# Eight PSUM banks shared out anew and a hand-written order re-timed in an attention-plus-FFN kernel

## The chip, the cores and the metric

The kernel runs on one core of a Trainium2 chip. The metric is the device time of one launch in microseconds (us), the median of the runs. Names of engines are those of the profile: PE is the matrix engine, PEld its weight load, DVE, ACT and POOL the vector, scalar and GpSimd engines, SP the queue that issues most of the DMAs here. L12 is line 12 of the kernel before, unless the text says that a line is of the changed one.

## The reference

Eight batches of eight heads, 1024 positions and head dimension 64 go through an attention with projected keys and values, and its output, as 8192 tokens of 512, through a feed-forward layer:

```
k_proj = np.einsum('ks,bhsd->bhkd', E, k)          # E, F: 64 x 1024
v_proj = np.einsum('ks,bhsd->bhkd', F, v)
attn   = softmax(q @ k_proj^T / sqrt(64))          # over the 64 projected keys
x      = (attn @ v_proj) as 8192 x 512
h      = x @ w_in                                  # 512 x 2048
g      = h * sigmoid(1.702 * h)
out    = g @ w_out                                 # 2048 x 512
```

## The kernel before, in words

The tokens are worked off in 16 blocks of 512 (two to a batch). For each block PE does FFN1, 16 tiles of 4 matmuls (`ffn1`, L412, matmul L418), each tile evacuated by ACT with the gelu (L420) into `gT`, and then FFN2. Block 0's FFN2 is plain (`ffn2`, L422). From block 1 on, FFN2 is done with seven products of half matrices in place of eight (`ffn2_parts`, L467, matmul L485): sums of halves of `w_out` are made once on DVE (`w_sums`, L446, tiles `tw`) and sums of halves of `gT` once a block on DVE (`g_sums`, L457, tiles `sg`). The seven products are 14 parts of 8 matmuls each, numbered 0 to 13 here. They accumulate in three banks of PSUM, `g0`, `g1`, `g2`: products 1 and 2 in `g0`, 6, 7 and 4 in `g1`, 5 and 3 in `g2`. Partial sums are taken out of a bank in the middle: after product 7 (part 9) DVE adds `g1` to a saved sum into the output tile (L528), and product 4, which comes next, goes on adding in the same bank, so that its first matmul must wait for that read.

The attention of later blocks is woven into this work: `scores` (matmul L266, exp on ACT L285), `sums` (the softmax denominators, matmul L304, copied to `den` by DVE L307), `gather` and `spread` (the denominators go through DRAM to be re-laid: den to `rc` L315, reciprocal L323, `rc` to `rdr` L325, `rdr` to `rbc` in two DMAs L328, all issued by SP), `values` (matmul at L266's helper, multiplied by `rbc` on DVE L350 into `xT`). For blocks 1 and 2 another form is used: `tok` (L390, reciprocal L395, multiply L397) and `x_tr` (transposes L405, copy L406). A batch's projection is `proj` (L177), its copies `kv_out` (L225 to L226: `k_b`, then a transposing DMA into `kt`), and `q_dma` (L256) transposes q by DMA. `load` issues a batch's k, v and q loads on POOL's queue; each of these tensors has one buffer, freed by the batch before.

PSUM has eight banks. `ps_f` has five buffers for all of FFN1, scores, sums, values, tok, x_tr and proj; `ps_g` has the three named banks. `f_tile` takes a `ps_f` buffer; until FFN2 of block 1 (the `opening`), `x_any` instead takes `g0`, `g1`, `g2` in turn for attention work.

Nothing is scheduled by a tool: the order is written by hand. `at(j, slot, f)` puts step f of the attention behind FFN1 tile `slot` of block j, or for slots from `O` (16) on, behind a part of FFN2 that the table `SLOT` (L637) names. Every engine and queue works through its instructions in this order; a step waits where its tile or buffer is not free.

## Time and profile before

| | us |
|---|---|
| median of 16 runs | 506.34 |
| lowest of the runs | 504.25 |
| the profiled execution's own time | 504.25 |
| its span, first to last instruction | 502.5 |
| PE busy | 484.2 |
| ACT busy | 275.5 |
| DVE busy | 202.6 |
| POOL busy | 81.0 |

The profiled execution is 2.1 us below the median, and 1.75 us of its time lie outside its span. A matmul's row in the timeline shows a start and a length; the lengths overlap, since matmuls are pipelined, so the distance between the starts of two rows tells more than the gap that is shown between them.

### The profile page before, as it was taken

How to read it: one execution, taken by the hardware profiler on the slowest of the kernel's cores; microseconds unless marked ns; L12 is line 12 of the kernel's file. 1: busy time of each engine (PE TensorE's matmuls, PEld its weight loads, DVE VectorE, ACT ScalarE, POOL GpSimd, SP SyncE). 2: the span in 40 equal slices, each digit the busy share in tenths (PEclk: the TensorE clock that was granted, in tenths of full speed). 3: DMA queues.
4: the chain of work that ended last, by engine and by line, in shares of the span. 5: the costliest groups of instructions: out<-in, count | busy, mean ns of one | idle time of the engine just before them, and what ended most of it. 6: DMA issues, size and time to landing. Idle time of an engine off the chain costs nothing.

```text
span 502.5 us, 8738 instructions
## 1 busy us (share of the span) xinstructions
PE 484.2 (96%) x3707; PEld 298.1 (59%) x3707; DVE 202.6 (40%) x434; ACT 275.5 (55%) x444; POOL 81.0 (16%) x100
## 2 busy tenths in 40 slices
PE   8999989997999999999999999999999999999996
PEld 4644447565475665747566574757557475756665
DVE  4413875334243444424243532433453242334241
ACT  1664364663656646575565646566465647554351
POOL 7562060320600330005100060000000000000000
PEclk9999999999999999999999999999999999999999
DMA  9999999999998999189982899447230505032202
GB/s 167 200 190 208 210 153 176 199 225 133 191 201 203 158 121 254 27 190 127 200 165 87 168 97 235 97 146 109 93 85 3 168 1 165 8 119 52 85 0 85
DMA packets 131548, 69.09 MB, mean 137 GB/s; under 512 B 98229, under 2 KB 122805, under 8 KB 129589
## 3 DMA queue, kind: packets, MB, share of 16 engines
q0 software_dynamic: 86496, 29.37, 53.7%
q1 hardware_dynamic: 44932, 38.90, 31.2%
q8 instruction: 29, 0.48, 0.4%
q10 hardware_dynamic: 80, 0.26, 0.3%
q14 instruction: 11, 0.08, 0.0%
HBM read 72.88 MB, written 16.99 MB: 179 GB/s over the span
## 4 chain that ended last, share of the span: by engine, by line
PE 83%; DMA 7%; DVE 5%; ACT 2%; issue 1%; POOL 1%; SPq 0%; DVEq 0%; POOLq 0%
PE f_ps L418 39%; PE g_ps L485 35%; PE f_ps L266 2%; PE f_ps L430 2%; DMA rbc<-rdr 2%; PE f_ps L177 2%; ACT expT L285 2%; DMA q_even<-in_q_dram 2%; DMA kt<-k_b 2%; DMA rdr<-rc 1%; DVE x_sb L397 1%; PE f_ps L304 1%; DVE o_sb L453 0%; DVE tw L454 0%; POOL k_sb L57 0%
## 5 line engine op out<-in xcount | busy, mean ns | idle before, releaser
L418 PE MATMUL f_ps<-xT,w_in_sb 128*128 128x512 bf16 (+1 forms) x1032 | 224.4, 377 | 0.0
L420 ACT ACTIVATE gT<-f_ps 128x512 bf16<-128x512 f32 (+1 forms) x258 | 153.2, 594 | 79.1 <-PE f_ps L418 78.9
L418 PEld LDWEIGHTS <-w_in_sb 128*128 128x128 bf16 x1032 | 100.7, 98 | 116.7 <-issue 0.8
L485 PEld LDWEIGHTS <-sg 128*128 128x128 bf16 x960 | 92.7, 98 | 16.2 <-DVE sg L465 5.2
L485 PE MATMUL g_ps<-tw,sg 128*128 128x256 bf16 x720 | 83.8, 273 | 0.0
L485 PEld LDWEIGHTS <-gT 128*128 128x128 bf16 x720 | 69.3, 98 | 17.3 <-issue 6.3
L462 DVE TENSOR_TENSOR sg<-gT 128x1024 bf16<-128x1024 bf16 (+2 forms) x45 | 23.0, 512 | 119.5 <-ACT gT L420 119.5
L69 POOL DMA_DIRECT2D q_sb<-in_q_dram x48 | 42.0, 906 | 167.2 <-DMA qT<-q_sb 141.7
L485 PE MATMUL g_ps<-w_out_sb,gT 128*128 128x256 bf16 x480 | 57.6, 273 | 0.0
L285 ACT ACTIVATE expT<-f_ps 128x512 bf16<-128x512 f32 (+1 forms) x60 | 31.6, 583 | 24.0 <-PE f_ps L266 23.8
L350 DVE TENSOR_TENSOR xT<-f_ps,rbc 128x512 bf16<-128x512 f32 x52 | 33.4, 684 | 26.9 <-DMA rbc<-rdr 19.6
L528 DVE TENSOR_TENSOR o_sb<-g_ps,u_sb 128x512 f32<-128x512 f32 x15 | 10.4, 691 | 64.1 <-PE g_ps L485 42.6
L533 ACT COPY o_sb<-g_ps 128x512 f32<-128x512 f32 x15 | 8.8, 585 | 41.2 <-PE g_ps L485 41.2
L485 PE MATMUL g_ps<-tw,gT 128*128 128x256 bf16 x240 | 28.8, 273 | 1.6 <-DVE o_sb L528 1.6
L485 PE MATMUL g_ps<-w_out_sb,sg 128*128 128x256 bf16 x240 | 28.6, 273 | 0.0
L507 ACT COPY u_sb<-g_ps 128x512 f32<-128x512 f32 x30 | 17.7, 589 | 14.4 <-ACT u_sb L507 8.1
L463 DVE TENSOR_TENSOR sg<-sg,gT 128x1024 bf16<-128x1024 bf16 (+2 forms) x45 | 23.1, 514 | 1.6
L538 DVE TENSOR_TENSOR o_sb<-g_ps,u_sb 128x512 f32<-128x512 f32 x15 | 10.4, 692 | 32.9 <-PE g_ps L485 32.9
L464 DVE TENSOR_TENSOR sg<-gT 128x1024 bf16<-128x1024 bf16 (+2 forms) x45 | 22.8, 506 | 0.0
L465 DVE TENSOR_TENSOR sg<-gT,sg 128x1024 bf16<-128x1024 bf16 (+2 forms) x45 | 22.8, 506 | 0.0
L289 ACT ACT_TABLE_LOAD x15 | 19.2, 1283 | 0.3
L499 ACT COPY g_ps<-g_ps 128x512 f32<-128x512 f32 x15 | 8.6, 570 | 18.6 <-PE g_ps L485 17.1
(103 smaller groups left out, 294.0 us busy)
## 6 DMA issues: line engine op xcount, KB each, us to landing
out_dram<-o_sb SPq DMA_DIRECT2D x15, 1024.0 KB, 4.1
rbc<-rdr SPq DMA_DIRECT2D x26, 512.0 KB, 7.3
k_sb<-in_k_dram POOLq DMA_DIRECT2D x7, 1024.0 KB, 13.1
v_sb<-in_v_dram POOLq DMA_DIRECT2D x7, 1024.0 KB, 18.1
q_sb<-in_q_dram POOLq DMA_DIRECT2D x48, 128.0 KB, 5.7
w_in_sb<-in_moe_w_in_dram POOLq DMA_DIRECT2D x8, 256.0 KB, 11.1
w_out_sb<-in_moe_w_out_dram POOLq DMA_DIRECT2D x4, 512.0 KB, 11.5
q_even<-in_q_dram POOLq DMA_DIRECT2D x12, 128.0 KB, 13.3
```

What stands on the lines that cost most here:

```text
L69: nc.gpsimd.dma_start(out=qt[b][:, j], in_=qv[:, j])
L285: nc.scalar.activation(expT[h][:, 2 * u + i, ts], s_ps[i], AF.Exp, scale=scale)
L289: nc.scalar.preload_act_table(AF.Gelu_apprx_sigmoid)
L350: nc.vector.tensor_tensor(x_of(h)[:, 2 * u + i, :], n_ps[i], rbc[h][:, 2 * u + i, :], op=ALU.mult)
L418: nc.tensor.matmul(h_ps, w_in_sb[:, kc, fc * P:(fc + 1) * P], xT[j][:, kc, ts], start=(kc == 0), stop=(kc == KC - 1))
L420: nc.scalar.activation(gts[j][:, fc, ts], h_ps, AF.Gelu_apprx_sigmoid)
L462: tt(t[0], g[:, lo, THI], g[:, hi, THI], op=ALU.add)
L463: tt(t[1], t[0], g[:, lo, TLO], op=ALU.subtract)
L464: tt(t[2], g[:, lo, TLO], g[:, lo, THI], op=ALU.subtract)
L465: tt(t[3], g[:, hi, TLO], t[1], op=ALU.subtract)
L485: nc.tensor.matmul(gb[bank[i]][:, tc_], a[:, k, tc_ * P:(tc_ + 1) * P], w[:, k], start=(first and tc_ == 0 and k == 0), stop=(final and k ...
L507: nc.scalar.copy(u[n], gb[n])
```

## The change

It shares out the banks anew. `ps_f` has four buffers in place of five, and there is a fourth named bank `g3`. In the opening `x_any` turns through four named banks in place of three. After the opening every fifth `f_tile` is `g3`, so that five banks still go round. The second of the two tiles of `sums` is now always `g0`.

It moves steps. The six DVE instructions of `w_sums`, all at block 1's tile 0 before, go one to block 0's piece 10, three to its last piece, two to block 1's tile 6. Block 2's `tok` and its `x_tr`, woven into block 1's FFN2, have two parts of FFN2 between them in place of one; batch 2's `q_dma` goes from part 7 of that FFN2 to part 6; `sums(3)` and `gather(3)` go from block 2's tile 3 to block 1's part 11, `spread(3)` from tile 6 to tile 0 and from SP's queue to POOL's; the loads of batch 3 go behind it. Batch 2's projection goes from tile 3 to tile 1 of block 2, batch 3's from block 2's FFN2 to block 3's tile 3, and its `q_dma` to block 3's tile 2. The slots from `O` on now count parts directly; `O + 1`, `O + 6`, `O + 9` and `O + 11` are the parts where `O`, `O + 3`, `O + 6` and `O + 7` were, so that most steps stay where they stood.

It changes the last block. Product 7 comes before the second half of product 2. Products 5 and 3 go, by halves of the tokens, into two `f_tile`s, and the last sum and its output are two pieces of 128 tokens.

The core of the diff:

```diff
-    ps_f = ctx.enter_context(tc.tile_pool(name="ps_f", bufs=5, space=PSUM))
+    ps_f = ctx.enter_context(tc.tile_pool(name="ps_f", bufs=4, space=PSUM))
...
+    opening, f_next, g_next = [True], [0], [0]
+
     def f_tile(shape, dt=F32):
+        if not opening[0]:
+            f_next[0] += 1
+            if f_next[0] % 5 == 0:
+                return ps_g.tile(shape, dt, name="g3_ps")
         return ps_f.tile(shape, dt, name="f_ps")
...
-        return ps_g.tile(shape, dt, name=f"g{g_next[0] % 3}_ps")
+        return ps_g.tile(shape, dt, name=f"g{g_next[0] % 4}_ps")
...
-            d_ps = [x_any([P, TB]) for _ in range(2)]
+            d_ps = [x_any([P, TB]), ps_g.tile([P, TB], F32, name="g0_ps")]
...
-    def spread(h):
+    def spread(h, q=nc.sync):
...
-            nc.sync.dma_start(out=rdr.rearrange("p e (r n) -> (p e r) n", n=n), in_=rc)
+            q.dma_start(out=rdr.rearrange("p e (r n) -> (p e r) n", n=n), in_=rc)
...
-                nc.sync.dma_start(out=rbc[h][r], in_=rdr[None, :, e, :].to_broadcast([D, HP, TB]))
+                q.dma_start(out=rbc[h][r], in_=rdr[None, :, e, :].to_broadcast([D, HP, TB]))
...
+        def p3l(tc_):
+            def go():
+                for k in range(FH):
+                    nc.tensor.matmul(gl[tc_][:, :MH], sg[:, 3, k, tc_ * P:(tc_ + 1) * P], b22[:, k],
+                                     start=False, stop=(k == FH - 1), skip_group_check=True)
+                nc.vector.tensor_tensor(o[:, tc_, MH:], gl[tc_][:, :MH], u[1][:, tc_], op=ALU.add)
+                put(slice(tc_, tc_ + 1), slice(MH, DM))
+            return go
...
+        if last:
+            return [p1a, p1b, p5l(0), p5l(1), h(6, 0), p6b, h(2, 0), h(7, 0), p7b, p2b, h(4, 0), p4b, p3l(0), p3l(1)]
...
-    at(1, 0, w_sums)
+    for i, f in enumerate(w_sums()):
+        at(*((0, Q + 10), (0, Q + 13), (0, Q + 13), (0, Q + 13), (1, 6), (1, 6))[i], f)
...
-    at(2, 3, sums(3), gather(3), proj(2), kv_out(2, nc.scalar.copy))
-    at(2, 6, spread(3))
...
+    at(1, O + 11, sums(3), gather(3))
+    at(1, O + 6, q_dma(2))
+    at(2, 0, spread(3, nc.gpsimd), lambda: load(3))
+    at(2, 1, proj(2), kv_out(2, nc.scalar.copy))
...
+    at(3, 2, q_dma(3))
+    at(3, 3, proj(3), kv_out(3))
...
-    SLOT = {1: 0, 3: 1, 5: 2, 6: 3, 7: 4, 8: 5, 9: 6, 11: 7}
```

**PE, behind part 9 of block 3's FFN2**, stands here with the buffers' numbers (weight loads and repeats left out); `f_ps` is a `ps_f` buffer, `g0_ps` and `g3_ps` are named banks. Before:

```order
L485 MATMUL g1_ps_1735<-tw_202,sg_203 128x256
L266 MATMUL f_ps_1834<-qT_1393,kt1_130 32x512
L266 MATMUL f_ps_1835<-qT_1393,kt1_130 32x512
L266 MATMUL f_ps_1846<-expT_1395,vq0_131 32x512
L266 MATMUL f_ps_1847<-expT_1395,vq0_131 32x512
L304 MATMUL f_ps_1858<-expT_1516,ones_137 32x512
L304 MATMUL f_ps_1859<-expT_1516,ones_137 32x512
L485 MATMUL g1_ps_1735<-tw_202,gT_1602 128x256
```

And in the changed kernel:

```order
L493 MATMUL g1_ps_1735<-tw_202,sg_203 128x256
L270 MATMUL g3_ps_1834<-qT_1603,kt1_130 32x512
L270 MATMUL f_ps_1835<-qT_1603,kt1_130 32x512
L270 MATMUL f_ps_1846<-expT_1393,vq0_131 32x512
L270 MATMUL f_ps_1847<-expT_1393,vq0_131 32x512
L308 MATMUL f_ps_1858<-expT_1514,ones_137 32x512
L308 MATMUL g0_ps_1859<-expT_1514,ones_137 32x512
L493 MATMUL g1_ps_1735<-tw_202,gT_1578 128x256
```

The order is the same. Before, six tiles went through five banks, so the sixth took the bank of the first, which ACT must have read; now the sixth is in `g0`.

**SP's queue, from block 1's FFN2 to block 3.** `qT`, `kt` are the transposing DMAs, `rc`, `rdr`, `rbc` the denominators' way, `out_dram` a block's output. Before:

```order
L256 DMA_TRANSPOSE qT<-q_even 128x32x128
L542 DMA out_dram<-o_sb 128x2048
L315 DMA rc<-den 128x1x32
L226 DMA_TRANSPOSE kt_129<-k_b 128x4x64
L325 DMA rdr<-rc 128x32
L328 DMA rbc<-rdr 64x4x512 x2
L256 DMA_TRANSPOSE qT<-q_sb 128x32x128
L315 DMA rc<-den 128x1x32
L226 DMA_TRANSPOSE kt_130<-k_b 128x4x64
L542 DMA out_dram<-o_sb 128x2048
```

And in the changed kernel:

```order
L260 DMA_TRANSPOSE qT<-q_even 128x32x128
L319 DMA rc<-den 128x1x32
L547 DMA out_dram<-o_sb 128x2048
L230 DMA_TRANSPOSE kt_129<-k_b 128x4x64
L319 DMA rc<-den 128x1x32
L547 DMA out_dram<-o_sb 128x2048
L329 DMA rdr<-rc 128x32
L332 DMA rbc<-rdr 64x4x512 x2
L260 DMA_TRANSPOSE qT<-q_sb 128x32x128
L230 DMA_TRANSPOSE kt_130<-k_b 128x4x64
```

Block 3's denominators (the first `rc`) are gathered ahead of block 1's output, and their `rdr` and `rbc` have left this queue. Batch 3's q transpose and `kt_130` now stand behind the next block's `rdr` and `rbc`.

**DVE, from the end of block 0 to batch 1's key copy.** `tw` and `o_sb` are the tiles of `w_sums`, `k_b` the copy of the projected keys. Before:

```order
L406 COPY xT<-g_ps 128x256 x2
L450 TENSOR_TENSOR tw<-w_out_sb 128x2048
L451 TENSOR_TENSOR tw<-w_out_sb 128x2048
L452 TENSOR_TENSOR o_sb<-w_out_sb 128x2048
L453 TENSOR_TENSOR o_sb<-o_sb,w_out_sb 128x2048
L454 TENSOR_TENSOR tw<-w_out_sb,o_sb 128x2048
L455 CAST tw<-o_sb 128x2048
L225 CAST k_b<-f_ps 64x512
```

And in the changed kernel, from the first of these sums on:

```order
L459 TENSOR_TENSOR tw<-w_out_sb 128x2048
L410 COPY xT<-g_ps 128x256 x2
L399 RECIPROCAL rd<-g_ps 128x4
L401 TENSOR_TENSOR x_sb<-g_ps,rd 128x256
...
L410 COPY xT<-g_ps 128x256 x2
L459 TENSOR_TENSOR o_sb<-w_out_sb 128x2048
L459 TENSOR_TENSOR tw<-w_out_sb 128x2048
L459 TENSOR_TENSOR o_sb<-o_sb,w_out_sb 128x2048
L229 CAST k_b<-f_ps 64x512
```

One sum stands ahead of the last two token copies of block 1, three behind them, and two (not shown) behind `k_b`.

## The prediction

> **What bounds the kernel now.** The page comes first, then PE's waits.

> ```profile
> PE 484.2 (96%) x3707; PEld 298.1 (59%) x3707; DVE 202.6 (40%) x434; ACT 275.5 (55%) x444; POOL 81.0 (16%) x100
> ```

> ```profile
> PE f_ps L304 <- ACT expT L285: 2.8, 10, 0.3
> ...
> PE f_ps L405 <- DVE x_sb L397: 1.0, 4, 0.3
> PE g_ps L266 <- ACT expT L285: 0.8, 2, 0.5
> PE g_ps L390 <- DVE xT L406: 0.5, 3, 0.2
> ```

> PE is the bound, and the change keeps its matmuls. So it can gain only what PE loses between them, and the second view names places: total, times, longest. These figures are too small: a matmul's row is drawn to its modelled end, and part of a wait lies under it. I therefore work from distances between starts, with 0.217 us for a matmul of 512 columns (the L418 group under rival 3: 224.4 us for 1032) and half of that for 256, so 0.87 for an FFN1 tile and for a part of FFN2.

> **The change part by part.** *Sums in `g0`, blocks 3 to 12.* PE behind part 9 of block 3 and of block 13 (which has no scores left to do), then of block 4, where a projection follows; start, length, what, count, idle before:

> ```profile
> 149.03 0.41 PE L266 MATMUL f_ps<-qT,kt 64*32 64x512 bf16 x8
> ...
> 150.12 0.41 PE L304 MATMUL f_ps<-expT,ones 64*32 64x512 bf16 x7 [0.28 <-ACT expT L285]
> 150.46 1.92 PE L485 MATMUL g_ps<-tw,gT 128*128 128x256 bf16 x16
> ...
> 439.43 0.41 PE L266 MATMUL f_ps<-expT,vq 64*32 64x512 bf16 x8
> ...
> 440.35 0.82 PE L485 MATMUL g_ps<-tw,gT 128*128 128x256 bf16 x6 [0.30 <-DVE o_sb L528]
> ```

> ```profile
> 178.37 0.41 PE L304 MATMUL f_ps<-expT,ones 64*32 64x512 bf16 x7 [0.28 <-ACT expT L285]
> 178.85 0.38 PE L177 MATMUL f_ps<-k_sb,eft 128*64 128x512 bf16 x1
> ```

> In block 3 the fill takes 150.46 - 149.03 = 1.43 us, because the sixth tile takes the bank of the first score tile and waits for its exp. With that tile in `g0`, whose last reader (the copy of product 2) is two parts back, the wait goes. What is late next is DVE's read of `g1`: block 13 has no exp wait, and product 4 still comes 440.35 - 439.43 = 0.92 us behind part 9. So a fill costs 0.92 and gains 0.51. There are ten such waits, 2.8 us in all, in blocks 3 to 12. In the four with a projection (4, 6, 8, 10) the projection is the sixth tile of the five banks and waits for the first exp, no longer the second: 178.85 less the start that the first exp allows, about 178.25 (where the row at 178.37 stands, whose wait that exp ends), gains 0.6. Sum: 6 x 0.51 + 4 x 0.6 = **5.5** (4.5 if the projections gain half of it; 6.1 if all ten gain 0.6).

> *Opening.* The two score waits on a named bank (0.8 us, 2) and the three of `tok` (0.5, 3) go with a fourth bank. The row behind one of them, and the sum that now stands ahead of two copies in DVE's queue:

> ```profile
> 39.84 0.40 PE L266 MATMUL g_ps<-qT,kt 64*32 64x512 bf16 x4 [0.48 <-ACT expT L285]
> ```

> ```profile
> 53.79 1.22 DVE L450 TENSOR_TENSOR tw<-w_out_sb 128x2048 bf16<-128x2048 bf16 x1
> ...
> 64.33 0.67 DVE L225 CAST k_b<-f_ps 64x512 bf16<-64x512 f32 x1
> ```

> I add 0.15 to each shown wait for what lies under the rows: 1.3 + 5 x 0.15 = 2.05. Against it, DVE reaches the last tokens' multiplies later; two pieces of FFN2 lie between, so of 1.22 us I let 0.4 show (bounds 0 and 1.22). Four `ps_f` banks in the opening cost nothing: a gelu takes less time than a tile's matmuls (rival 3). **1.65** (0.8 to 2.3).

> *The wait for batch 1's keys.* PE, and SP's queue:

> ```profile
> 71.00 1.91 PE L485 MATMUL g_ps<-w_out_sb,gT 128*128 128x256 bf16 x16
> 74.29 0.62 PE L266 MATMUL f_ps<-qT,kt 64*32 64x512 bf16 x16 [1.38 <-DMA kt<-k_b]
> ...
> 89.84 3.62 PE L418 MATMUL f_ps<-xT,w_in_sb 128*128 128x512 bf16 x16
> ...
> 112.81 0.40 PE L266 MATMUL f_ps<-qT,kt 64*32 64x512 bf16 x4
> 116.16 0.40 PE L266 MATMUL f_ps<-qT,kt 64*32 64x512 bf16 x4 [2.95 <-DVE xT L350]
> 116.75 0.41 PE L266 MATMUL f_ps<-expT,vq 64*32 64x512 bf16 x8 [0.20 <-DVE xT L350]
> ...
> 125.73 13.98 PE L418 MATMUL f_ps<-xT,w_in_sb 128*128 128x512 bf16 x64
> ```

> ```profile
> 57.67 5.26 SPq L256 DMA_TRANSPOSE qT<-q_sb  x1
> 65.02 1.84 SPq L226 DMA_TRANSPOSE kt<-k_b  x1
> ...
> 84.30 7.43 SPq L256 DMA_TRANSPOSE qT<-q_even  x1
> ...
> 95.18 0.70 SPq L315 DMA_DIRECT2D rc<-den  x1
> ...
> 104.03 1.32 SPq L328 DMA_DIRECT2D rbc<-rdr  x2
> ```

> `k_b` (64.33) stood behind all six sums; now it comes at once. But SP is busy with q's transpose until 57.67 + 5.26 = 62.93, so `kt` can go out at most 2.1 us sooner, while PE arrives 1.65 sooner. With the same time in flight the wait shrinks by 0.45. **0.5** (0 to 1.5, the whole wait, 74.29 - 71.00 - 16 x 0.109).

> *Block 2's tokens.* Each of the four visits in block 1's FFN2 waits for DVE:

> ```profile
> 82.91 0.28 PE L405 MATMUL f_ps<-ident,x_sb 128*128 128x128 bf16 x2
> 83.45 0.28 PE L405 MATMUL f_ps<-ident,x_sb 128*128 128x128 bf16 x2 [0.26 <-DVE x_sb L397]
> ```

> The second pair starts 0.54 behind the first and needs some 0.11, so 0.4 is lost, four times: 1.6. With two parts between, the multiplies are done. But behind part 9 the new order puts two transposes, a `tok` and all of `scores(3)` in a row on five banks, behind L528 in DVE's queue; I take 0.3 off. **1.3** (0.6 to 1.7).

> *Block 3's values.* The rows at 112.81, 116.16 and 116.75 show block 2's PE waiting for a bank that the `values` multiply holds until `rbc` lands: four of these matmuls take 0.11, so 116.16 - 112.92 and 116.75 - 116.27 less 0.1, together **3.6**. The sums now come two parts ahead of block 2 and not four tiles into it: 6 x 0.87 = 5.2 us sooner against PE's work. But SP transposes batch 2's q first, from 84.30 (when that q has landed) for 7.43 us, so `rc` cannot go before 91.7 less the 1 us by which I take that q to land sooner: 90.7 against 95.18, 4.5 sooner, while PE is 3.45 sooner (the three parts above). That alone leaves 2.5 of the wait. But from `rc` to `rbc` it took 104.03 - 95.18 = 8.9 while batch 3's loads ran; they now stand behind, and I estimate 6. So the wait goes, and three small ones come: product 4's DVE wait in block 2, whose fill loses its projection (0.37, by block 13's rows); the projection of batch 2 at tile 1 meeting its v load; DVE's copies behind the reciprocal. For v, its issue and its time to landing:

> ```profile
> 76.80 0.87 POOL L57 DMA_DIRECT2D v_sb<-in_v_dram  x1 [1.27 <-PE g_ps L485]
> ...
> 95.94 0.88 POOL L57 DMA_DIRECT2D k_sb<-in_k_dram  x1 [18.27 <-PE f_ps L177]
> ```

> ```profile
> v_sb<-in_v_dram POOLq DMA_DIRECT2D x1, 1024.0 KB, 11.9
> ```

> It landed at 88.7; PE now arrives at 89.84 - 3.45 + 2 x 0.87 = 88.1, with the load itself some 1 us sooner. I take 0.3 for it, 0.3 for the copies, 0.4 for batch 3's projection (rival 2). 3.6 - 1.4 = **2.2** (0 to 3.6).

> [...]

> ```profile
> L69 POOL DMA_DIRECT2D q_even<-in_q_dram x12: 873/890/1513, 19.8 to 74.6; - x12
> ```

> One issue took 1513 ns against a median of 890. [...]

> *Last block.* PE waits for L528 between products 7 and 4, and the last sum spans 512 columns:

> ```profile
> 494.89 1.91 PE L485 MATMUL g_ps<-tw,gT 128*128 128x256 bf16 x16 [0.84 <-DVE o_sb L528]
> ...
> 498.58 0.69 DVE L538 TENSOR_TENSOR o_sb<-g_ps,u_sb 128x512 f32<-128x512 f32 x1 [3.75 <-PE g_ps L485]
> ```

> ```profile
> out_dram<-o_sb SPq DMA_DIRECT2D x15, 1024.0 KB, 4.1
> ...
> out_dram<-o_sb SPq DMA_DIRECT2D x4, 256.0 KB, 2.3
> ```

> Product 2's second half, 8 matmuls, now covers DVE's 0.69: 0.84 gained. The last sum halves, 0.35. The last transfer halves from 256 KB; on a line through the two sizes shown that is worth 1.8 x 128 / 768 = 0.3 (bounds 0 and 1.15). **1.5** (0.8 to 2.3).

> **Sum.** 5.5 + 1.65 + 0.5 + 1.3 + 2.2 + 1.5 = 12.65. The profiled execution took 504.25 us (span 502.5): 491.6. It lies 2.1 below the median of 506.34; the same gain there gives **493.7**.

> **Rivals.** *1. The loads keep the clock.* The gains before block 3 are worth something only if the DMAs come earlier too. Batch 2's q and v follow `proj(1)`, but they also share the engines with everything else; if they land at the same time as before, the gains up to block 2's start (3.45) are lost again at its projection and its `rc`, and what stays is 5.5 + 1.5 + some 1.3 of block 2: 8.3, **498**. For it: `kt` and v both show PE within 1 us of a landing. Against: v's issue hangs on PE's `proj(1)` through POOL's order.

> *2. Batch 3 is late.* POOL now issues batch 3's loads behind `rbc(3)`, 3 to 6 us later than at 95.94, and its projection is needed at block 3's tile 3:

> ```profile
> v_sb<-in_v_dram POOLq DMA_DIRECT2D x1, 1024.0 KB, 17.3
> ```

> From about 98 to 102, plus 17.3, plus up to 3.5 for `rbc`'s own megabyte ahead of it, v lands at 115 to 123; PE is there at about 121.3 (block 3 began at 125.73; less 3.45, the 2.6 that block 2 saves by then and the projection's 16 x 0.109, plus four tiles). Then come q's transpose and `kt(3)`, behind `rdr(4)` and `rbc(4)` on SP, and `scores(6, 0)` wants them some 25 us into block 3. Price 3 to 5 us: **498**. [...]

> *3. Slower.* With four banks in the opening FFN1 could wait for ACT in blocks 0 and 1. A tile's matmuls take 4 x 0.217 = 0.87 us and a gelu 0.59:

> ```profile
> L418 PE MATMUL f_ps<-xT,w_in_sb 128*128 128x512 bf16 (+1 forms) x1032 | 224.4, 377 | 0.0
> L420 ACT ACTIVATE gT<-f_ps 128x512 bf16<-128x512 f32 (+1 forms) x258 | 153.2, 594 | 79.1 <-PE f_ps L418 78.9
> ```

> To eat 12.65 us, each of 34 tiles would have to lose 0.37, that is, a bank's round trip would have to exceed 4 x 0.87 = 3.5 us. At 0.8 a tile 34 x 0.8 = 27 less 12.65 makes **521**. The rows give a round trip near 0.87 + 0.59 and some hand-over, about 1.7 us, so it decides only far from here.

> *4. The exp itself is awaited.* If `sums` waited for its data and not its bank, the 5.5 would not come: **499.2**. Its exps are a block old, so no.

> **How the numbers follow.** Forecast 0.68, rival 1 0.15, rival 2 0.10, rival 3 0.03, rival 4 0.03, small rest 0.01. The parts' upper bounds add to 17.1, but not all at once; I take 16 for the low end, 490.3. The high end takes in rivals 1 and 2 and part of the parts' low ends: 498.7. A measurement of this kernel can tell about 0.2%, 1 us, from no change. Faster 0.95, within 0.2% 0.02, slower 0.03.

> **What would show it.** Right: no PE wait on `expT` behind part 9 of blocks 3 to 12, product 4 waiting there for DVE alone; no wait for `xT` in block 2; no 0.84 in the last block; blocks 3 and 5 some 0.5 shorter. Wrong: waits of PE's projections (L181 of the changed kernel) or first scores of block 3 for DMAs of several us, or FFN1 waiting for ACT in blocks 0 and 1.

## The result and the profile after

| | before | after |
|---|---|---|
| median of the runs, us | 506.48 (48 runs) | 491.18 (9 runs, 490.70 to 491.35) |
| the profiled execution's own time, us | 504.25 | 491.25 |
| its span, us | 502.5 | 489.5 |
| PE busy, us | 484.2 | 479.6 |

The ratio of the two is 0.9697, with a 95% interval of 0.968 to 0.9713. The forecast was 493.7 (490.3 to 498.7). The spans differ by 13.0 us, the medians by 15.3.

What PE waits for in the kernel after (total, times, longest; three of 0.2 to 0.4 us are left out):

```profile
PE g_ps L150 <- DVE u_sb L115: 1.5, 1, 1.5
PE f_ps L189 <- DMA k_sb<-in_k_dram: 1.3, 1, 1.3
PE g_ps L493 <- DVE o_sb L536: 1.1, 3, 0.5
PE f_ps L181 <- ACT expT L289: 0.8, 3, 0.3
...
PE g_ps L270 <- DVE xT L410: 0.3, 1, 0.3
...
```

The ten waits of the sums, those for `kt`, for `xT` in block 2 and for `x_sb` are gone. FFN1 (L422) waits for ACT nowhere. Lines are those of the kernel after.

To place the gain I cut both executions at the first FFN1 matmul of a block. Each row is a stretch; its second figure is the length, the third figure from the end the granted clock. First before, then after: block 0, 1, 2, 3, blocks 4 to 12, the last block (blocks 13 and 14 are left out).

```profile
22.17:55.02 32.85, 31.89 (x202) 16.24 (x201) 8.85 (x29) 16.85 (x29) 14.22 (x17) 1.00 1.50 195
55.02:89.84 34.82, 32.47 (x258) 19.92 (x257) 23.64 (x47) 19.63 (x32) 9.38 (x10) 1.00 1.62 181
89.84:125.73 35.89, 32.74 (x267) 19.25 (x264) 14.73 (x28) 18.53 (x31) 8.75 (x10) 1.00 1.38 185
125.73:153.97 28.24, 27.96 (x219) 17.51 (x216) 10.95 (x21) 17.09 (x28) 8.75 (x10) 1.00 1.41 198
153.97:416.13 262.16, 259.33 (x2011) 162.27 (x2008) 103.98 (x201) 153.82 (x244) 26.28 (x30) 1.00 0.72 128
...
471.34:502.50 31.16, 26.36 (x178) 17.13 (x175) 7.61 (x15) 12.46 (x21) 0.00 (x0) 0.97 0.18 68
```

```profile
22.90:54.06 31.16, 31.16 (x202) 16.07 (x201) 10.03 (x29) 16.85 (x29) 13.11 (x16) 1.00 1.47 197
54.06:87.09 33.03, 32.56 (x266) 20.35 (x265) 23.36 (x49) 19.74 (x32) 10.37 (x11) 1.00 1.74 185
87.09:117.44 30.35, 30.05 (x242) 18.15 (x240) 11.90 (x23) 18.42 (x30) 10.60 (x13) 1.00 1.23 201
117.44:147.10 29.66, 29.59 (x235) 18.26 (x233) 12.50 (x24) 17.10 (x28) 8.75 (x10) 1.00 1.20 158
147.10:404.61 257.51, 256.14 (x2010) 161.77 (x2008) 103.74 (x201) 153.83 (x244) 26.29 (x30) 1.00 0.79 138
...
459.82:489.50 29.68, 26.34 (x178) 17.09 (x175) 7.77 (x16) 12.62 (x22) 0.00 (x0) 1.00 0.19 72
```

Block 0 is 1.69 shorter, block 1 1.79, blocks 2 and 3 together 4.12, blocks 4 to 12 together 4.65, the last 1.48; 13 and 14 take 55.21 together in both. Against this the first block starts 0.73 later, at the mercy of the first loads: over the profiles of all the kernels below it starts between 21.8 and 23.7. The sum is 13.0.

PE in block 2 of the kernel after, at the place of the old wait for `rbc`, and DVE's first multiply by `rbc`:

```profile
109.75 0.41 PE L270 MATMUL f_ps<-qT,kt 64*32 64x512 bf16 x8
```

```profile
105.39 0.69 DVE L354 TENSOR_TENSOR xT<-g_ps,rbc 128x512 bf16<-128x512 f32 x1 [0.38 <-PE f_ps L270]
```

The scores' two tiles follow each other (one row of eight matmuls, where before there were two rows with 3.35 us between their starts), and DVE waits for PE and not for the DMA.

### The profile page after: what moved, and what is told of

It reads as the page before. It is cut to its first block, busy times and chain, and to the rows that moved or that the text cites. A ratio compares the mean times of both kernels' runs of the same rounds, so it can differ in the third digit from the quotient of the medians.

```text
span 489.5 us, 8743 instructions
## 1 busy us (share of the span) xinstructions
PE 479.6 (98%) x3707; PEld 297.7 (61%) x3707; DVE 202.0 (41%) x435; ACT 275.7 (56%) x445; POOL 83.0 (17%) x103
## 4 chain that ended last, share of the span: by engine, by line
PE 91%; DMA 2%; DVE 2%; issue 2%; ACT 2%; POOL 1%; DVEq 0%; ACTq 0%; POOLq 0%
PE f_ps L422 37%; PE g_ps L493 35%; PE g_ps L422 8%; PE f_ps L434 3%; PE f_ps L181 2%; DMA q_even<-in_q_dram 2%; PE f_ps L270 2%; DVE o_sb L536 1%; ACT expT L289 1%; PE g_ps L270 1%; ACT o_sb L531 1%; POOL k_sb L57 0%; PE g_ps L181 0%; PE f_ps L552 0%; PE f_ps L562 0%
## 5 line engine op out<-in xcount | busy, mean ns | idle before, releaser
L422 PE MATMUL f_ps<-xT,w_in_sb 128*128 128x512 bf16 (+1 forms) x856 | 193.2, 377 | 0.0
L422 PEld LDWEIGHTS <-w_in_sb 128*128 128x128 bf16 x1032 | 100.5, 98 | 117.0 <-issue 1.2
L424 ACT ACTIVATE gT<-f_ps 128x512 bf16<-128x512 f32 (+1 forms) x214 | 126.9, 593 | 69.9 <-PE f_ps L422 69.7
L493 PEld LDWEIGHTS <-sg 128*128 128x128 bf16 x928 | 89.5, 98 | 16.0 <-DVE sg L473 5.2
L493 PE MATMUL g_ps<-tw,sg 128*128 128x256 bf16 x704 | 82.1, 273 | 0.0
L69 POOL DMA_DIRECT2D q_sb<-in_q_dram x48 | 42.0, 905 | 159.5 <-DMA qT<-q_sb 135.1
L422 PE MATMUL g_ps<-xT,w_in_sb 128*128 128x512 bf16 x176 | 45.2, 379 | 0.0
L289 ACT ACTIVATE expT<-f_ps 128x512 bf16<-128x512 f32 (+1 forms) x50 | 26.7, 580 | 16.7 <-PE f_ps L270 13.5
L536 DVE TENSOR_TENSOR o_sb<-g_ps,u_sb 128x512 f32<-128x512 f32 x15 | 10.4, 692 | 62.0 <-PE g_ps L493 37.3
L354 DVE TENSOR_TENSOR xT<-f_ps,rbc 128x512 bf16<-128x512 f32 x40 | 26.2, 684 | 20.3 <-DMA rbc<-rdr 14.1
L424 ACT ACTIVATE gT<-g_ps 128x512 bf16<-128x512 f32 x44 | 26.3, 597 | 12.2 <-PE g_ps L422 12.2
L493 PE MATMUL g_ps<-w_out_sb,sg 128*128 128x256 bf16 x224 | 26.7, 273 | 0.0
L515 ACT COPY u_sb<-g_ps 128x512 f32<-128x512 f32 x29 | 17.1, 590 | 12.6 <-ACT u_sb L515 8.1
## 6 DMA issues: line engine op xcount, KB each, us to landing
out_dram<-o_sb SPq DMA_DIRECT2D x15, 1024.0 KB, 3.9
k_sb<-in_k_dram POOLq DMA_DIRECT2D x7, 1024.0 KB, 13.7
v_sb<-in_v_dram POOLq DMA_DIRECT2D x7, 1024.0 KB, 18.1
w_in_sb<-in_moe_w_in_dram POOLq DMA_DIRECT2D x8, 256.0 KB, 10.3
```

Of the source, the lines that this page charges most:

```text
L69: nc.gpsimd.dma_start(out=qt[b][:, j], in_=qv[:, j])
L289: nc.scalar.activation(expT[h][:, 2 * u + i, ts], s_ps[i], AF.Exp, scale=scale)
L354: nc.vector.tensor_tensor(x_of(h)[:, 2 * u + i, :], n_ps[i], rbc[h][:, 2 * u + i, :], op=ALU.mult)
L422: nc.tensor.matmul(h_ps, w_in_sb[:, kc, fc * P:(fc + 1) * P], xT[j][:, kc, ts], start=(kc == 0), stop=(kc == KC - 1))
L424: nc.scalar.activation(gts[j][:, fc, ts], h_ps, AF.Gelu_apprx_sigmoid)
L493: nc.tensor.matmul(gb[bank[i]][:, tc_], a[:, k, tc_ * P:(tc_ + 1) * P], w[:, k], start=(first and tc_ == 0 and k == 0), stop=(final and k ...
```

## The experiments

Median times, with that of the kernel before in the same comparison in brackets.

**1. The sums' bank alone (g0_alone).** In the kernel before, one line:

```diff
-            d_ps = [x_any([P, TB]) for _ in range(2)]
+            d_ps = [x_any([P, TB]), ps_g.tile([P, TB], F32, name="g0_ps")]
```

> The kernel before with one line changed: the second tile of the sums is in g0 (five ps_f buffers stay, nothing else is moved). Theory (the sixth tile waited for a bank): the ten waits on an exp behind part 9 of blocks 3 to 12 go, and the time falls by 5.2 us, what blocks 3 to 12 gained in the two traces (six times 0.54 and four times 0.49), to about 501.2. Rival (the sums wait for their exps themselves, or product 4 waits as long for the read of g1): no change, 506.4.

Measured: 501.05 (506.68), ratio 0.9885, interval 0.9859 to 0.9911. In its trace blocks 4, 6, 8 and 10 take 29.75 us and the others from 5 to 11 take 27.70, as in the kernel after (30.24 and 28.24 before). The wait was for the bank. The rival falls.

**2. All of the banks, none of the order (banks_alone).** As 1, with `ps_f` of four, `g3` as every fifth `f_tile`, and

```diff
-        return ps_g.tile(shape, dt, name=f"g{g_next[0] % 3}_ps")
+        return ps_g.tile(shape, dt, name=f"g{g_next[0] % 4}_ps")
```

> The kernel before with the whole change to the banks and none to the order: four ps_f buffers, g3 as every fifth f_tile after the opening, four named banks in turn in the opening, the sums' second tile in g0. Theory: the opening's waits on a bank go with the fourth named bank whatever DVE's order is, so it is another 1.7 us faster than with g0 alone, about 499.5. Rival (the opening's gain came from the weight sums' new places, or four ps_f buffers cost what the fourth named bank gives): as with g0 alone, 501.2.

Measured: 499.55 (506.68), ratio 0.9846, interval 0.9813 to 0.9879. Block 0 takes 31.03 us: the opening's 1.8 come from the fourth bank alone. But the trace shows more. From block 0's start to block 3's it takes 125.97 - 22.13 = 103.8 us, and 125.73 - 22.17 = 103.6 before: by block 3 the 1.8 are gone again. PE comes to block 2's wait for `rbc` 1.9 sooner (110.87 against 112.81) and leaves it only 1.0 sooner (115.21 against 116.16), and the rest goes at half clock behind it (115.17 to 118.58). So the agreement of the median, with an interval as wide, is no proof that the opening's gain reaches the end.

**3. The weight sums at their old place (wsums_back).** In the kernel after:

```diff
-        at(*((0, Q + 10), (0, Q + 13), (0, Q + 13), (0, Q + 13), (1, 6), (1, 6))[i], f)
+        at(1, 0, f)
```

> The changed kernel with all six weight sums at block 1's tile 0 again, ahead of the copy of the keys. Theory of the trace after (the keys' copy behind the sums was the whole cause of the wait for kt): the wait comes back with 1.45 us, less 0.15 that the sum ahead of the last token copies costs now: 492.5. Rival, as in the prediction (SP's transpose of q bounds the keys' DMA, and the sums' place is worth 0.5 less the same 0.15): 491.5.

Measured: 491.14 (506.68), ratio 0.9697, interval 0.9667 to 0.9727; the kernel after has 491.18. The theory's 492.5 falls. The rival's 491.5 can't be told from no change, with runs from 490.88 to 492.38. The sums' places are worth nothing that can be measured. PE behind part 1 of block 1, first here, then in experiment 2, where the sums also stand at their old place:

```profile
71.00 0.63 PE L270 MATMUL f_ps<-qT,kt 64*32 64x512 bf16 x16
```

```profile
72.37 0.62 PE L271 MATMUL f_ps<-qT,kt 64*32 64x512 bf16 x16 [1.31 <-DMA kt<-k_b]
```

PE begins part 0 at the same time in both (69.16 and 69.14), and SP's queue issues the transpose into `kt` at 63.17 and 63.35. Once it is there in time, 6.6 us behind its issue, and once 1.4 us late, 9.0 behind it by PE's start. In experiment 1, the same code as before up to this place, the wait is 0.1 us at most. So whether PE waits here is decided by that DMA's time in flight, which differs between these executions. What decides that is open.

**4. Block 3's sums at their old place (sums3_back).** In the kernel after:

```diff
-    at(1, O + 11, sums(3), gather(3))
...
-    at(2, 0, spread(3, nc.gpsimd), lambda: load(3))
-    at(2, 1, proj(2), kv_out(2, nc.scalar.copy))
+    at(2, 3, sums(3), gather(3), proj(2), kv_out(2, nc.scalar.copy))
+    at(2, 6, spread(3))
...
-        if j % NB2 == 0 and j // NB2 + 2 < B and j != 2:
+        if j % NB2 == 0 and j // NB2 + 2 < B:
```

> The changed kernel with block 3's sums and gather at block 2's tile 3 again, with the projection of batch 2, and the spread at tile 6 on SP, the loads of batch 3 ahead of it at the block's start. Theory (block 2 gained by the earlier rbc): the wait for rbc before block 2's last products comes back, 3.4 us in the two traces: 494.5. Rival (it was PE's three parts of earlier progress, or the loads, that set it; these stay): under 1 us, 491.2 to 492.

Measured: 498.81 (506.68), ratio 0.9845, interval 0.9816 to 0.9875: 7.6 us slower than the kernel after, twice what I had expected. The step is worth more than the trace of before showed. PE, DVE and the stretches around the wait; in the last rows the third figure from the end is the granted clock:

```profile
109.98 0.40 PE L270 MATMUL f_ps<-qT,kt 64*32 64x512 bf16 x4
114.97 0.61 PE L270 MATMUL f_ps<-qT,kt 64*32 64x512 bf16 x4 [4.59 <-DVE xT L354]
...
117.62 2.67 PE L493 MATMUL g_ps<-tw,sg 128*128 128x256 bf16 x16
```

```profile
113.63 0.69 DVE L354 TENSOR_TENSOR xT<-g_ps,rbc 128x512 bf16<-128x512 f32 x1 [8.39 <-DMA rbc<-rdr]
```

```profile
112.00:114.00 2.00, 0.00 (x0) 0.00 (x0) 0.37 (x1) 0.00 (x0) 0.00 (x0) 0.59 3.11 150
114.00:116.00 2.00, 1.03 (x13) 0.20 (x13) 1.23 (x3) 0.37 (x1) 0.87 (x1) 0.50 3.26 146
116.00:118.00 2.00, 2.00 (x13) 1.44 (x11) 0.98 (x2) 0.36 (x2) 0.00 (x0) 0.50 3.57 146
118.00:120.00 2.00, 2.00 (x15) 1.56 (x13) 0.00 (x0) 0.45 (x1) 0.00 (x0) 0.71 1.22 47
```

PE came to this place 2.8 us sooner than before (109.98 against 112.81), and left it only 1.2 sooner (114.97 against 116.16): `rbc` lands only 1.8 sooner (DVE's first multiply by it begins at 113.63, before at 115.41), and the wait, now 4.9 us, swallows most of what was gained ahead of it. And behind it the clock is at half: the sixteen matmuls of 256 columns at 117.62, 1.75 us elsewhere, take 2.6. From 114.97 to where the clock is back (118 + 2 x 0.58 = 119.2, if it was 0.5 before and 1 after) half of 4.2 us is lost, 2.1. The wait of 4.9 and these 2.1 are 7.0 of the 7.6.

**5. and 6. Useless work in the wait (before_busy, before_busy15).** In the kernel before, ahead of `scores(4, 1)` in block 2, ten (then fifteen) matmuls that add zeros to the open bank `g2`:

```diff
+    def busy(n):
+        def go():
+            for _ in range(n):
+                nc.tensor.matmul(live[2].rearrange("p i m -> p (i m)"), zeros[:, :P], zeros,
+                                 start=False, stop=False, skip_group_check=True)
+        return go
...
-    at(2, O + 3, scores(4, 1), values(3, 1))
+    at(2, O + 3, busy(10), scores(4, 1), values(3, 1))
```

> The kernel before with ten useless matmuls of 512 columns (2.2 us) in block 2's FFN2 ahead of scores(4, 1), where PE then waits 3.2 us for a bank that rbc holds; they add zeros to the open bank g2, so nothing that is computed changes. Theory (in most runs of the kernel before that wait is long enough to halve PE's clock for some us behind it, which the profiled execution, 2.2 us below the median, just escaped): the work lies inside the wait and keeps the clock, and the median falls to that of the profiled execution, 504.3. Rival (the clock has no part in it, and the spread of the runs is the DMAs'): no change, 506.5, or up to 2 us more where the work doesn't fit into the wait.

> As before_busy, with fifteen useless matmuls (3.3 us) in place of ten. [...]

Measured: 505.12 (506.56), ratio 0.9974, interval 0.995 to 0.9998, with ten; 504.29 (506.75), ratio 0.996, interval 0.9941 to 0.9979, with fifteen, where 504.8 and no run above 506.5 were expected. With ten, the mean granted clock of nine of the twelve runs is 0.998 or more (504.6 to 505.9 us), of three 0.995 to 0.997 (507.1 to 507.5). With fifteen it is 0.999 or 1.0 in all twelve, and none is above 506.4; the seventeen runs of the kernel before beside them have 0.992 to 0.998. The kernel becomes 2.5 us faster by 3.3 us of work that does nothing. A mean clock of 0.995 over 506 us is at most 2.5 us of full-speed time lost, which agrees in size (at most, since half clock costs nothing while PE is idle). The rival of no effect falls. The profiled execution of before, on which the prediction was made, had escaped at this place: its clock falls only at 500.6, behind its last matmul, which makes its mean 0.998. No kept trace of the kernel before shows the half clock itself; that of experiment 1, the same order up to here, shows it from 116.5 to 119.9, right behind this wait.

**7. The spread on SP (spread_sp).** In the kernel after:

```diff
-    at(2, 0, spread(3, nc.gpsimd), lambda: load(3))
+    at(2, 0, spread(3), lambda: load(3))
```

> The changed kernel with block 3's spread issued by SP and no longer by POOL; the loads of batch 3 stay at their place, and so no longer wait behind rbc. Theory (from rdr to rbc it takes some 6 us, and from rbc's issue to its landing 8, while the loads run, as in the kernel before and with the sums at block 2's tile 3): rdr goes at 93.3, rbc at 99.6, and PE, which is there at 109.9, waits until some 112.2: 2.3 us slower, 493.5. Rival (the loads' place behind rbc is worth nothing, or SP's DMAs pass them): no change, 491.2.

Measured: 502.45 (506.56), ratio 0.9916, interval 0.9884 to 0.9948: 11.3 us slower than after, where I had 2.3. SP's queue and PE:

```profile
93.81 0.33 SPq L329 DMA_DIRECT2D rdr<-rc  x1
101.84 1.32 SPq L332 DMA_DIRECT2D rbc<-rdr  x2
103.25 1.85 SPq L230 DMA_TRANSPOSE kt<-k_b  x1
```

```profile
103.38 1.91 PE L493 MATMUL g_ps<-w_out_sb,gT 128*128 128x256 bf16 x16
113.50 0.63 PE L270 MATMUL f_ps<-qT,kt 64*32 64x512 bf16 x8 [8.21 <-DMA kt<-k_b]
```

`rbc` must wait for `rdr` to land, SP waits with it, and the transpose into `kt` stands behind: it goes at 103.25 (91.86 in the kernel after). I had put `rbc` nearly right (99.6, it was 101.8) and not looked at what is queued behind it. PE stands idle for 8.4 us here, from 105.1 to 113.5, and until 117.8 its clock is at half, which loses another 2.1: 10.5 of the 11.3.

**8. The spread on SP behind that transpose (spread_sp_kt).**

```diff
-    at(2, 0, spread(3, nc.gpsimd), lambda: load(3))
-    at(2, 1, proj(2), kv_out(2, nc.scalar.copy))
+    at(2, 0, lambda: load(3))
+    at(2, 1, proj(2), kv_out(2, nc.scalar.copy), spread(3))
```

> As spread_sp, but with block 3's spread one tile later on SP, behind batch 2's projection and the transpose into kt, so that this transpose no longer stands behind rbc in SP's queue. Theory (of the 11.3 us that spread_sp lost, the most was kt held up behind rbc, which waits for rdr's landing; the rest of POOL's worth is that batch 3's loads stand behind rbc): kt goes at 92, rbc still lands near 112, PE waits for it some 2 to 3 us in block 2: 494. Rival A (POOL's place was worth only SP's order): 491.2. Rival B (rbc between the loads is so late that it loses as much as kt did): 500 or more.

Measured: 498.14 (506.75), ratio 0.9843, interval 0.9812 to 0.9875. `kt` is in time, and the old wait is back, with the halved clock (0.993 to 0.997 in its runs). PE, then DVE:

```profile
114.31 0.40 PE L270 MATMUL f_ps<-qT,kt 64*32 64x512 bf16 x4 [4.89 <-DVE xT L354]
```

```profile
112.97 0.69 DVE L354 TENSOR_TENSOR xT<-g_ps,rbc 128x512 bf16<-128x512 f32 x1 [8.68 <-DMA rbc<-rdr]
```

The sums are as early here as in the kernel after, and it gains hardly anything over experiment 4 (498.81). So it is not the sums' place that shortens `rbc`'s way but that batch 3's loads stand behind it. In the kernel after POOL issues, in this order:

```profile
93.57 0.57 POOL L329 DMA_DIRECT2D rdr<-rc  x1 [16.46 <-DVE rc L327]
96.53 1.24 POOL L332 DMA_DIRECT2D rbc<-rdr  x2 [2.38 <-DMA rdr<-rc]
97.77 0.91 POOL L57 DMA_DIRECT2D k_sb<-in_k_dram  x1
```

From `rdr` to `rbc` it takes 3.0 us, against 8.0 in experiment 7 and 6.4 before, where the loads run meanwhile. POOL's queue as such is not needed for that. SP's queue later in the kernel after shows both cases: first more than 22 us after the last issue of a load (the slowest load of k or v landed after 21.9), then behind a batch's loads, issued by POOL from 222.44 to 232.89:

```profile
205.94 0.38 SPq L329 DMA_DIRECT2D rdr<-rc  x1
209.64 1.26 SPq L332 DMA_DIRECT2D rbc<-rdr  x2
...
235.71 0.46 SPq L329 DMA_DIRECT2D rdr<-rc  x1
244.63 1.28 SPq L332 DMA_DIRECT2D rbc<-rdr  x2
```

It takes 3.7 us without the loads and 8.9 beside them. My theory had the mechanism and half of the price: 2 to 3 us of wait were 4.9 plus the clock.

**9. to 11. What is left behind part 9.** First (p7_first), product 7 ahead of product 2 in all blocks, with the sums and projections moved to part 11:

```diff
-        return [p1a, p1b, p5a, p5b, h(6, 0), p6b, h(2, 0), p2b, h(7, 0), p7b,
+        return [p1a, p1b, p5a, p5b, h(6, 0), p6b, h(2, 0), h(7, 0), p7b, p2b,
...
-            at(j, O + 9, sums(j + 2), gather(j + 2))
+            at(j, O + 11, sums(j + 2), gather(j + 2))
...
-            at(j, O + 9, proj(j // NB2 + 2), kv_out(j // NB2 + 2))
+            at(j, O + 11, proj(j // NB2 + 2), kv_out(j // NB2 + 2))
```

> The changed kernel with product 7's second half ahead of product 2's in every block, as it is in the last one; scores and values stand behind product 2 as before, and the sums, the gather and the projection move from part 9 to part 11. Theory (what is left behind part 9 is product 4's wait for DVE's read of g1, and in the even blocks the projection's wait for the first exp): the wait goes under product 2's eight matmuls. Gains from the trace after: 0.15 in each of the odd blocks 3 to 11 with a full fill, 0.37 in blocks 2 and 12, 0.55 in 13, 0.84 in 14, and 0.3 in each of the four with a projection: 4.1 together, 487.1. Rival (the sums behind part 11 wait for the copy of g0, or the gather comes too late for the next block's values): no gain, 491.2 or above.

Measured: 491.67 (506.56; 490.27 to 493.43), ratio 0.9705, interval 0.9673 to 0.9738: nothing gained. The theory falls in most blocks. PE in block 13:

```profile
428.45 1.04 PE L493 MATMUL g_ps<-w_out_sb,gT 128*128 128x256 bf16 x8
429.41 0.40 PE L270 MATMUL f_ps<-expT,vq 64*32 64x512 bf16 x4
...
429.75 1.92 PE L493 MATMUL g_ps<-tw,gT 128*128 128x256 bf16 x16
```

Product 4 waits for nothing now. But eight matmuls from 428.45 end at 429.32, and eight of attention from 429.41 at 429.63: 0.1 goes on each side at the change between 64-row and 128-row matmuls, and a second piece of attention, the sums behind part 11, pays it again. Blocks 5, 7, 9 and 11 take 27.81 to 28.14 instead of 27.70, and block 2 takes 31.18 instead of 30.35, with a wait of 0.4 for batch 2's v load (30.85 in experiment 3, whose edit leaves block 2 alone). Only block 14, which has no sums, gains what was forecast: 26.93 against 27.50.

Then (p7_first_s3), in addition, block 3's scores apart from the tokens, behind parts 4 and 8 of block 1's FFN2:

```diff
-        at(1, O + 9, scores(3, u))
+        at(1, O + 4 + 4 * u, scores(3, u))
```

> As p7_first, and block 3's scores in block 1's FFN2 no longer both behind part 9 but behind parts 4 and 8. Theory (in the trace after, scores(3) took 1.43 us instead of 0.45 because four tiles of it, two token tiles and two transposes came in a row on five banks): another 0.9 us, 486.2. Rival (the wait only moves to the sums of block 3 behind part 11, or to rbc in block 2): as p7_first, 487.1.

Measured: 493.76 (506.56), ratio 0.9744, interval 0.9708 to 0.9779: slower, by something that neither theory had. q's second transpose is not done by then:

```profile
74.00 1.04 PE L493 MATMUL g_ps<-tw,sg 128*128 128x256 bf16 x8
77.29 0.63 PE L270 MATMUL f_ps<-qT,kt 64*32 64x512 bf16 x8 [2.26 <-DMA qT<-q_sb]
77.85 1.89 PE L493 MATMUL g_ps<-tw,sg 128*128 128x256 bf16 x8
```

The eight matmuls at 77.85, 0.87 us at full speed, take 1.7: the clock is at half here too, after some 2.4 us of idleness.

Last (three_small), three moves that these traces allow, in the kernel after: product 7 first in block 14 alone, the projection ahead of the sums in the even blocks, the scores of block 3 behind parts 6 and 8.

```diff
+        mid = [h(2, 0), h(7, 0), p7b, p2b] if j == NBLK - 2 else [h(2, 0), p2b, h(7, 0), p7b]
...
-        at(1, O + 9, scores(3, u))
+        at(1, O + 6 + 2 * u, scores(3, u))
...
+        if j % NB2 == 0 and j // NB2 + 2 < B:
+            at(j, O + 9, proj(j // NB2 + 2), kv_out(j // NB2 + 2))
         if j + 2 < NBLK:
             at(j, O + 9, sums(j + 2), gather(j + 2))
```

> The changed kernel with three small moves: in block 14 alone product 7's second half ahead of product 2's (0.57 in p7_first's trace), in blocks 4, 6, 8 and 10 the projection ahead of the sums (it waited 0.3 for the first exp as the sixth tile; now the sums' first tile is the sixth, 1.7 us later: 4 x 0.3 = 1.2), and block 3's scores behind parts 6 and 8 of block 1's FFN2, later than where p7_first_s3 had to wait for q's transpose (up to 0.9). Theory: all three come, 488.5. Rival (each fill that is split costs PE two more changes between 64-row and 128-row matmuls, 0.1 each, and the tokens' DVE work stands behind scores(3) anyway): 0.57 + 1.2 alone, 489.4; with nothing from the projections, 490.6.

Measured: 489.54 (506.75; four runs, 489.31 to 489.75), ratio 0.9668, interval 0.9638 to 0.9698. It beats the kernel after by 1.6 (the two intervals overlap, the ranges of their runs do not), where 2.7 were hoped for. Block 14 takes 26.94 (0.56 less), blocks 4, 6, 8 and 10 take 29.55 (0.2 less each, not 0.3). Block 1 gains nothing: 33.06 against 33.03. The scores no longer queue for banks, but with them gone the fill behind part 9 is short, as in block 13, and no longer covers DVE's read of `g1`. DVE begins that read as soon as PE has finished product 7, and product 4 waits for it. PE, then DVE:

```profile
82.06 1.91 PE L493 MATMUL g_ps<-tw,gT 128*128 128x256 bf16 x16 [0.39 <-DVE o_sb L536]
```

```profile
81.31 0.69 DVE L536 TENSOR_TENSOR o_sb<-g_ps,u_sb 128x512 f32<-128x512 f32 x1 [1.00 <-PE g_ps L493]
```

## Why the prediction was right, point by point

**The sums in `g0`**, 5.5: right. 0.54 in block 3, 4.65 in blocks 4 to 12, together 5.2; alone on the kernel before (experiment 1) they make all of it. Behind part 9 of a block with a full fill, and of block 13, PE now goes:

```profile
142.92 0.40 PE L270 MATMUL f_ps<-expT,vq 64*32 64x512 bf16 x8
...
143.61 1.58 PE L493 MATMUL g_ps<-tw,gT 128*128 128x256 bf16 x13
...
427.91 0.40 PE L270 MATMUL f_ps<-expT,vq 64*32 64x512 bf16 x4
...
428.83 1.91 PE L493 MATMUL g_ps<-tw,gT 128*128 128x256 bf16 x16 [0.30 <-DVE o_sb L536]
```

The forecast "product 4 waiting there for DVE alone" holds only where the fill is short: block 13 shows it, a full fill (block 3) covers DVE's read. In the even blocks the projection waits 0.3 for the first exp, as the step said; those blocks gained 0.49 and not 0.6.

**The opening**, 1.65: right. Block 0 is 1.69 shorter; experiment 2 gives 1.8 for the fourth bank, and the sum ahead of the last copies costs the rest.

**The keys**, 0.5: the size failed, and the working. The wait (1.45) is gone. The step let `kt` go 2.1 us sooner and PE come 1.65 sooner, with the same time in flight. `kt` went 2.4 sooner (62.62 against 65.02), but PE came only 0.95 sooner (part 0 at 70.05 against 71.00), since the first block began 0.73 later. That alone takes the 1.45: with the 9.2 us in flight of before `kt` would have landed at 71.8, just when PE came for it. It took 7.5. Experiment 3 shows that the sums' place, which the step was about, does not matter, so that the whole wait is gone is luck as far as this step goes.

**Block 2's tokens**, 1.3: mis-sized. The four waits went (1.6), but `scores(3)` behind them took 1.43 us, where it took 0.91 before, and the first tokens, which now come two parts sooner, wait some 0.4 for their exps, a wait that the step did not have. So 0.7 came; I had let 0.3 show for five banks and eight tiles. The first tokens:

```profile
74.57 0.29 PE L394 MATMUL g_ps<-vx,expT 128*128 128x130 bf16 x2 [0.21 <-ACT expT L289]
```

**Block 3's values**, 2.2: mis-sized. Blocks 2 and 3 gave 4.12; less the 0.54 of block 3's own sums and the 0.35 that `sums(3)` took with it to block 1, 3.2. Of the four small waits that I had set against the 3.6, product 4's 0.37 came; those for v, for DVE's copies and for batch 3's projection did not. That the one for v stayed away is luck of this execution: with nearly the same order up to there, PE waits 0.9 for it in the profile of experiment 7 and 0.4 in that of experiment 9. The estimate of 6 us from `rc` to `rbc` was right (90.58 to 96.53), and experiment 8 shows that it hangs on the loads not running beside it. `spread(3)`'s three issues on POOL took 0.57, 0.62 and 0.63 us; what made one q load's issue take 1.51 in the trace of before no run shows.

**The last block**, 1.5: right, 1.48.

The terms as measured make 5.2 + 1.7 + 1.45 + 0.7 + 3.2 + 1.5 = 13.75; the later start takes 0.73 off; 13.0 on the spans, against 12.65 forecast. That the sum comes so near is in part luck: the keys and block 3's values brought 0.95 and 1.0 more than their terms, the tokens and the sums 0.6 and 0.3 less, and the late start took back the 0.73 that the keys' surplus owes to it. The parts' upper bounds add to 17.5 and not to 17.1; nothing hangs on it.

**"The same gain there" for the median** is the step that failed, and it holds nearly all of the miss of 2.5 us. The profiled execution had lain 2.1 below the median and I took that for chance. Experiments 5 and 6 show that it is PE's clock, halved in most runs behind block 2's wait, and the change takes away that wait: its runs have 0.999 or 1.0. The length of the wait alone does not settle it: idle for 3.2 us in the profiled execution of before, PE kept its clock; idle for 3.8 in experiment 1 and 4.9 in experiment 4 it lost it; and in p7_first_s3 2.4 us were enough. What the traces show of it stands in the last section.

**The rivals.** 1 (loads keep the clock) did not come, but its mechanism is real: in experiments 2 and 4 most of what was gained up to block 2 is given back, since PE leaves the wait there only 1.0 and 1.2 us sooner, and at the half clock behind it. The change gains what it gains ahead of block 3 only because it moves that landing too. 2 (batch 3 late) did not come: no projection and no score of batch 3 waits. 3 and 4 fell.

## What to carry to other kernels

Where PE waits for a DMA, take the gains ahead of that place for nothing until the landing itself is sooner, and then count them all at once (in experiments 2 and 4 PE came 1.9 and 2.8 us sooner to such a wait and left it 1.0 and 1.2 sooner). How long a small DMA takes that is waited for depends here on the loads that run beside it (from `rdr` to `rbc` 3.0 and 3.7 us without, 6.4 to 8.9 with them in the cases of experiment 8) more than on when its data are ready; and what stands behind it in its own queue pays for its wait (the transpose into `kt` went at 103.25 and not at 91.86 in experiment 7, and PE stood idle for 8.4). A profiled execution below the median of its runs is a sign to look at the granted clock of the others.

## What the runs showed of the hardware

```profile
73.43:76.84 3.41, 1.40 (x14) 0.93 (x12) 1.12 (x4) 2.22 (x5) 1.47 (x2) 1.00 1.81 156
76.84:80.25 3.41, 2.96 (x23) 2.04 (x24) 0.26 (x2) 1.50 (x3) 0.00 (x0) 0.50 3.09 148
```

```profile
111.45:114.87 3.42, 1.76 (x18) 1.14 (x16) 0.00 (x0) 1.18 (x2) 0.23 (x1) 1.00 1.60 191
114.87:118.28 3.41, 1.92 (x23) 1.28 (x23) 2.37 (x4) 0.70 (x2) 0.65 (x1) 1.00 2.99 150
```

Behind a full-clock piece in which PE was busy for 1.44 us or less, the next was at half clock (1.40 here, 1.44 at 108.93 to 112.34 in experiment 4, 1.38 at 497.16 to 500.57 before). Behind one with 1.64 us or more it was not (1.76 and 1.92 here, 1.64 at 107.79 to 111.20 in experiment 8). None of the 145 full-clock pieces of the profiled execution of before is an exception. Where between 1.44 and 1.64 the border lies, and whether PE's busy time alone decides, these runs don't show. It does answer what the lengths of the waits left open: of p7_first_s3's wait, 2.26 us by its row, 1.8 lie in one piece, with another wait of 0.2 beside them; the one of before, 2.95 by its row, is cut by a border of the grid into 1.7 and 1.3.

A change between matmuls of 64 and of 128 rows cost PE about 0.1 us each way (0.09 and 0.12 in the rows of p7_first); what in it takes the time is not shown.
